# A start in source order, and two batches that take turns over the blocks of a hidden layer

## The chip, the cores and the metric

The kernel runs on one core of a Trainium2 chip. The metric is the device time of one execution in microseconds. The core's engines work beside each other, each through a queue of its own that it executes in order: TensorE (PE, matmuls; PEld in the profile is its weight load), VectorE (DVE), ScalarE (ACT), GpSimd (POOL) and SyncE (SP), which only issues transfers here. Results of PE land in PSUM, and DVE or ACT must copy them out before PE can use them as operands.

## The reference

Two softmax attentions and a two-layer network with Mish, cut to what matters (`_attn_ref`, `_moe_ref`):

```python
def sm_attn(qq, kk, vv):                     # q, k, v: 8 x 8 x 576 x 64;  p: 8 x 8 x 32 x 64
    s = scale * np.matmul(qq, kk.transpose(0, 1, 3, 2))
    s = s - np.max(s, axis=-1, keepdims=True)
    a = np.exp(s)
    a = a / (np.sum(a, axis=-1, keepdims=True) + 1e-09)
    return np.matmul(a, vv)
p_packed = sm_attn(p, k, v)                  # 32 packed rows for each batch and head
out = sm_attn(q, p_packed, p_packed)
x = out.transpose(0, 2, 1, 3).reshape(4608, 512)
h = x @ w_in                                 # 512 x 2048
g = h * np.tanh(softplus(h))
return g @ w_out                             # 2048 x 512
```

The two weights come as float64 and have to be made float32 on the chip.

## The kernel before

**Attention.** A `Batch` object holds one of the 8 batches; its 8 heads are worked in two groups g of four. `start` and `score` transpose p and k (PSUM tile `ps_kq`) and form the first scores `ps_s`; `exps` sums the exponentials into `rs`; `turn` transposes q into `qT`; `turn_weights` transposes the weights into `a1T`; `values` gives `ps_pp`, and `turn_values` its transpose `ppT`. `match` multiplies qT with ppT and transposes the result on DVE in squares of 32 (L240). `weigh` (L248 to L264) does the second softmax and leaves its transposed weights as a high and a low float32 part, `aT_hi` (ACT, L263) and `aT_lo` (DVE, L264). The generator `attention` yields these steps one by one, and the main loop slips a step between matmuls of the network.

**Folding.** The second attention's values are never formed: `packed_w(b, c)` multiplies ppT of batch b with chunk c of w_in (four chunks of 512 columns; PSUM tiles `ps_w`), which gives `wp_hi` (ACT, L349) and `wp_lo` (DVE, L350). The up-projection then multiplies aT with wp.

**Network.** The 2048 columns of the hidden layer are 16 blocks f of 128. A main-loop step t belongs to one block of one batch. `up(hf)` computes a half of the block's h transposed (288 of the batch's 576 rows): six matmuls into `ps_h`, three products (hi·hi, lo·hi, hi·lo) for each head group. ACT applies Mish (`g`, L391), and `halves` splits g into `g_hi`, `g_lo` on DVE (L400, L401). `down(grp, c)` adds the block's share to one of four accumulators `acc` (128 rows each) in three matmuls (L405 to L407). It runs two steps behind (`LAG`). The last 64 rows of a batch are kept in `g_rest` and multiplied with those of the next batch (`down_rest`).

**Weights.** `from_double` turns 128 x 512 float64 numbers to float32: SP stages them in `w_st` (three buffers), ACT makes the scaled high word and the low word (L295, L296), DVE joins them in four operations (L297, L298, L299, L302). There are 16 such pieces of w_in (`load_wi(c, m)`, four for each chunk) and 16 of w_out (`load_wo(i)`, which also splits them into `wo_hi` on ACT, L312, and `wo_lo` on DVE, L313). Chunks of w_in are written back as float32, and `fetch_wi` reads them again for later batches.

**Order.** PE executes in source order (`manual_schedule`). On the other engines a scheduler chooses the order when the kernel is built, and it is fixed from then on. The batches come one after the other: batch 0's attention runs first and alone, with the conversions placed among it, then t = 0 to 15 are batch 0's blocks, 16 to 31 batch 1's. Batch 1's attention is slipped in from t = 2 and completed at t = 14, where its first `packed_w` stands.

Of the kernel before, what the change touches and what calls it, by code (L numbers as in the profile page):

```python
# [10 lines left out]
I32 = mybir.dt.int32  # L11
# [8 lines left out]
W2K = 5  # L20

# [7 lines left out]
def body(  # L29
# [84 lines left out]
    def transposed(pool, src, g, dst):  # L114
        for i in range(NI):
            ps = psum(pool, [P, 4, R], "ps_kq")
            for h in range(4):
                nc.tensor.transpose(out=ps[:, h, :], in_=of_slot(src, g, h)[:, i, :], identity=ident[:R, :R])  # L118
            evacuate(dst[:, i, :, :], ps, i if pool is ps_acc else None)
            yield  # L120
# [15 lines left out]
    class Batch:  # L136
# [5 lines left out]
        def load(self):  # L142
            b = self.b
            self.k_t = [load_heads(k, b, g, "k_t") for g in range(2)]
            self.p_t = att.tile([P, 2, 2, D], F32, name="p_t", bufs=1)
            p_src = p[b].rearrange("(g h) n d -> (h n) g d", g=2)
            for u in range(2):
                nc.sync.dma_start(out=self.p_t[:, :, u, :], in_=p_src)
            self.q_t = [load_heads(q, b, g, "q_t") for g in range(2)]
            self.v_t = [load_heads(v, b, g, "v_t") for g in range(2)]  # L150
# [35 lines left out]

        def exps(self, gs):
# [41 lines left out]
        def turn(self, g, pool):  # L229
            self.qT[g] = att.tile([P, NI, 4, R], F32, name="qT", tag="T", bufs=2)  # L230
            yield from transposed(pool, self.q_t[g], g, self.qT[g])
# [11 lines left out]
        def weigh(self, gs):  # L243
            n = gs.stop - gs.start
            G = n * (S // NP)
            a2 = self.a2[:, gs].rearrange("a h g n -> a (h g) n")
            mx = stat.tile([P, 2 * (S // NP)], F32, name="mx2")[:, :G]
# [4 lines left out]
            nc.scalar.activation(out=a2, in_=a2, func=AF.Exp, scale=scale)  # L252
            sm = stat.tile([P, 2 * (S // NP)], F32, name="sm2")[:, :G]
# [14 lines left out]
        def attention(self):  # L268
# [15 lines left out]
            for g in range(2):  # L284
                yield from self.match(g, ps_a)
            self.weigh(slice(0, 2))

    def from_double(dst, src):


        x = src.rearrange("p (n t) -> p n t", t=2)
        low, high = x[:, :, 0], x[:, :, 1]
        bits = dst.bitcast(I32)
        r = wts.tile([P, dst.shape[1]], I32, name="wround", tag="w2k", bufs=W2K)
        nc.scalar.activation(out=dst, in_=high.bitcast(F32), func=AF.Copy, scale=F64_SCALE)  # L295
        nc.scalar.activation(out=r, in_=low.bitcast(U32), func=AF.Copy, scale=2.0 ** -29)  # L296
        nc.vector.tensor_scalar(out=dst, in0=dst, scalar1=F64_HIGH, scalar2=-F64_HIGH, op0=ALU.min, op1=ALU.max)  # L297
        nc.vector.tensor_scalar(out=bits, in0=bits, scalar1=3, scalar2=None, op0=ALU.logical_shift_left)  # L298
        nc.vector.scalar_tensor_tensor(  # L299
            out=bits, in0=high, scalar=-0x80000000, in1=bits, op0=ALU.bitwise_and, op1=ALU.bitwise_or  # L300
        )
        nc.vector.tensor_tensor(out=bits, in0=bits, in1=r, op=ALU.add)  # L302

    def staged(src):
        st = wts.tile([P, 2 * DO], I32, name="w_st", tag="wstage", bufs=3)
        nc.sync.dma_start(out=st, in_=src)
        return st

    def load_wo(i):
        w = wts.tile([P, DO], F32, name="wo32", tag="w2k", bufs=W2K)  # L310
        from_double(w, staged(w_out_v[:, i, :]))
        nc.scalar.copy(out=wo_hi[i], in_=w)  # L312
        nc.vector.tensor_tensor(out=wo_lo[i], in0=w, in1=wo_hi[i].bitcast(F32), op=ALU.subtract)  # L313
# [3 lines left out]
    def load_wi(c, m):  # L317

        g = m // 2
        if m % 2 == 0:  # L320
            wis[0, c, g] = wts.tile([P, 2, FC], F32, name="wi", tag="w32", bufs=4)
        from_double(wis[0, c, g][:, m % 2], staged(w_in_v[:, m, c * 2 * FC:(c + 1) * 2 * FC]))
        if m % 2:
            nc.sync.dma_start(out=w_in_f32[c][:, g], in_=wis[0, c, g])

    def fetch_wi(b, c):
        for g in range(2):
            wis[b, c, g] = wts.tile([P, 2, FC], F32, name="wi", tag="w32", bufs=4)
            nc.sync.dma_start(out=wis[b, c, g], in_=w_in_f32[c][:, g])

    def packed_w(b, c):
# [3 lines left out]
        for h in range(4):  # L335
            for g in range(2):
# [4 lines left out]
                    rhs=wis[b, c, g][row:row + D, h // 2, :],  # L341
# [24 lines left out]
    class Group:  # L366


        def __init__(self, b, f, wp, g_rest):
            self.b, self.f, self.wp, self.g_rest = b, f, wp, g_rest  # L370

        def tiles(self):
            self.act = moe.tile([P, MAIN], F32, name="g", tag="g", bufs=3)
            if self.f % 4 == 0:
                self.g_rest[self.b % 2].append(
                    moe.tile([P, 4, REST], F32, name=f"g_rest{self.b % 2}", bufs=2 if self.b % 2 else 5)
                )

        def up(self, hf):
# [12 lines left out]
            if m < HALF:  # L392
                nc.scalar.activation(
                    out=self.g_rest[self.b % 2][self.f // 4][:, self.f % 4, :], in_=ps[:, m:], func=AF.Mish
# [14 lines left out]
    def evac(acc, c):  # L409
        o = wts.tile([P, DO], F32, name="o", tag="w2k", bufs=W2K)  # L410
        if c % 2 == 0:
# [7 lines left out]
    def down(grp, c):  # L419
        b, f, g = grp.b, grp.f, grp.g  # L420
        if f == 0 and c == 0:
            accs[:] = [ps_acc.tile([P, DO], F32, name=f"acc{i}", tag="acc") for i in range(NCH)]
        down_one(accs[c], g[0], g[1], slice(c * P, (c + 1) * P), f, f == 0, f == NF - 1)
        if f < NF - 1:
            return
        o = evac(accs[c], c)
# [10 lines left out]
    def down_rest(grp):  # L437

        i = grp.f // 4
# [34 lines left out]
    with tc.manual_schedule(engines={mybir.EngineType.PE}):
# [3 lines left out]
        first.load()  # L478
        convert(2)
        first.start(ps_a)  # L480
        together(first.score(0, ps_acc))
        first.exps(slice(0, 1))
        together(first.score(1, ps_acc))
        first.exps(slice(1, 2))
        together(first.turn(0, ps_a))
        convert(2)
        together(first.turn_weights(0, ps_acc))
        together(first.turn(1, ps_a))
        together(first.turn_weights(1, ps_acc))
        together(first.values(0, ps_acc), first.values(1, ps_acc))  # L490
        together(first.turn_values(0, ps_a), first.turn_values(1, ps_a))
        together(first.match(0, ps_acc), first.match(1, ps_acc))
        for g in range(2):
            first.weigh(slice(g, g + 1))
        wps = {(0, 0): packed_w(0, 0)}
        convert(5)
# [3 lines left out]
        g_rest = None  # L500
        for t in range(n_groups + LAG):
            b, f = divmod(t, NF)
            grp = None
            if t < n_groups:
                if f == 0:
                    if b % 2 == 0:
                        g_rest = ([], [])
                if f == (0 if b else 2) and b + 1 < B:
                    gen = batches[b + 1].attention()
                if f == 10 and b + 2 < B:  # L510
                    batches[b + 2].load()
                grp = Group(b, f, wps[b, f // 4], g_rest)
# [3 lines left out]
            if b == 0:  # L516
                convert(2)
# [12 lines left out]
            if dn and dn.b % 2 == 1 and dn.f % 4 == 2:  # L530
                rest["g"] = split(dn.g_rest[0][dn.f // 4], dn.g_rest[1][dn.f // 4])
            if dn:
                down(dn, 3)
            if grp and f % 4 == 2:
                nb, nch = divmod(b * (NF // 4) + f // 4 + 1, NF // 4)
                if nb < B:
                    if nb > b:
                        together(gen)
                    wps[nb, nch] = packed_w(nb, nch)
                    if nb + (nch + 1) // 4 and nb + (nch + 1) // 4 < B:  # L540
                        fetch_wi(nb + (nch + 1) // 4, (nch + 1) % 4)
# [30 lines left out]
```

## Time and profile before

| what | value |
|---|---|
| median of 3 runs | 821.87 us (821.23 to 822.18) |
| the profiled execution | 822.64 us |
| its span | 820.9 us |
| busy: PE, DVE, ACT | 768.2, 420.6, 336.0 us |
| matmuls executed | 5584 |
| read and written in memory | 75.50 MB, 13.63 MB |

The span is the time from the profile's first event to its last; the execution's own time includes what lies around it. All instants (us) below are counted from the span's start. In rows of instructions the columns are start, duration, engine, line, operation, output and inputs, shapes, and in brackets the idle time ahead of it and what ended it. Rows of groups give busy time and mean ns of one. In rows of the chain of waits the second number is what that piece contributes.

### The profile page before, as it was taken

To read this page: it belongs to the slowest core of one execution; us is meant where nothing else is said; L and a number is where in the kernel's file an instruction comes from. 1 tells how busy PE (TensorE), PEld (TensorE's weight loads), DVE (VectorE), ACT (ScalarE), POOL (GpSimd) and SP (SyncE) were. 2 spreads that over 40 slices of the span, in tenths; PEclk is the share of its full clock that TensorE was granted. 3 is DMA by queue.
4 is the path that set the end of the run, shared out by engine and by line. 5 is a ranking of instruction groups with operands and counts; after the bars stand their busy time and mean duration, and the time that the engine had idled before them with its cause. 6 is when DMAs were issued, how large, how long until landed. Compare 5 with 4: busy or idle time off the path is not lost.

```text
span 820.9 us, 13745 instructions
## 1 busy us (share of the span) xinstructions
PE 768.2 (94%) x5584; PEld 610.4 (74%) x5584; DVE 420.6 (51%) x812; ACT 336.0 (41%) x766; POOL 0.7 (0%) x6
## 2 busy tenths in 40 slices
PE   6607789999999999999999999999999999999997
PEld 4406667787788787877778787877778787888886
DVE  4799895744373435544373435544373445533332
ACT  3557583435242353235242353335242353332221
POOL 0000000000000000000000000000000000000000
PEclk6557789999999999999999999999999999999999
DMA  9967673144311533144411433144311421131002
GB/s 256 287 226 231 207 243 95 52 139 138 110 52 52 143 95 111 52 138 139 110 52 52 132 107 111 52 137 140 110 52 52 122 67 53 52 103 52 1 1 64
DMA packets 43966, 90.02 MB, mean 110 GB/s; under 512 B 8576, under 2 KB 27008, under 8 KB 43904
## 3 DMA queue, kind: packets, MB, share of 16 engines
q1 hardware_dynamic: 43904, 89.15, 35.8%
q8 instruction: 44, 0.72, 0.4%
q14 instruction: 18, 0.15, 0.1%
HBM read 75.50 MB, written 13.63 MB: 109 GB/s over the span
## 4 chain that ended last, share of the span: by engine, by line
PE 88%; DMA 5%; DVE 4%; issue 1%; ACT 1%; SPq 0%; ACTq 0%
PE ps_h L388 25%; PE acc L405 16%; PE acc L407 14%; PE acc L406 14%; PE ps_kq L118 4%; DMA w_st<-in_moe_w_in_dram 4%; PE ps_w L338 4%; PE ps_s L127 3%; PE ps_rest L405 2%; PE ps_rest L407 2%; PE ps_rest L406 2%; PE ps_pp L209 1%; PE ps_a L200 1%; DMA k_t<-in_k_dram 1%; DMA w_st<-in_moe_w_out_dram 1%
## 5 line engine op out<-in xcount | busy, mean ns | idle before, releaser
L405 PE MATMUL acc<-wo_hi,g_hi 128*128 128x512 f32 x512 | 216.5, 423 | 0.0
L391 ACT ACTIVATE g<-ps_h 128x288 f32<-128x288 f32 (+1 forms) x256 | 98.5, 385 | 286.5 <-PE ps_h L388 250.5
L407 PE MATMUL acc<-wo_hi,g_lo 128*128 128x512 f32 x512 | 203.4, 397 | 0.0
L406 PE MATMUL acc<-wo_lo,g_hi 128*128 128x512 f32 x512 | 203.3, 397 | 0.0
L388 PE MATMUL ps_h<-aT_hi,wp_hi 128*128 128x288 f32 x512 | 159.3, 311 | 21.8 <-ACT aT_hi L263 21.1
L400 DVE CAST g_hi<-g 128x512 fp32r<-128x512 f32 x128 | 54.5, 426 | 239.7 <-ACT g L391 239.7
L388 PE MATMUL ps_h<-aT_lo,wp_hi 128*128 128x288 f32 x512 | 153.2, 299 | 1.9 <-DVE aT_lo L264 1.9
L388 PE MATMUL ps_h<-aT_hi,wp_lo 128*128 128x288 f32 x512 | 153.3, 299 | 0.0
L405 PEld LDWEIGHTS acc<-wo_hi,g_hi 128*128 128x128 f32 x512 | 97.4, 190 | 42.7 <-issue 20.4
L388 PEld LDWEIGHTS ps_h<-aT_hi,wp_hi 128*128 128x128 f32 x512 | 98.1, 192 | 39.6 <-ACT aT_hi L263 23.2
L407 PEld LDWEIGHTS acc<-wo_hi,g_lo 128*128 128x128 f32 x512 | 96.9, 189 | 23.7 <-DVE g_lo L401 0.2
L388 PEld LDWEIGHTS ps_h<-aT_lo,wp_hi 128*128 128x128 f32 x512 | 98.4, 192 | 11.3 <-DVE aT_lo L264 2.5
L406 PEld LDWEIGHTS acc<-wo_lo,g_hi 128*128 128x128 f32 x512 | 97.6, 191 | 8.6
L388 PEld LDWEIGHTS ps_h<-aT_hi,wp_lo 128*128 128x128 f32 x512 | 98.4, 192 | 0.0
L401 DVE TENSOR_TENSOR g_lo<-g,g_hi 128x512 fp32r<-128x512 f32 x128 | 88.2, 689 | 5.9
L350 DVE TENSOR_TENSOR wp_lo<-ps_w,wp_hi 128x512 fp32r<-128x512 f32 x64 | 41.3, 682 | 19.0 <-ACT wp_hi L349 19.0
L349 ACT CAST wp_hi<-ps_w 128x512 fp32r<-128x512 f32 x64 | 34.3, 588 | 32.8 <-PE ps_w L338 32.8
L338 PE MATMUL ps_w<-wi,ppT 64*32 64x512 f32 x512 | 35.7, 615 | 0.0
L118 PE MATMUL ps_kq<-ident,k_t 96*128 96x96 f32 x192 | 27.0, 273 | 9.0 <-issue 4.9
L118 PEld LDWEIGHTS ps_kq<-ident,k_t 96*128 96x128 f32 x192 | 23.1, 158 | 16.4 <-issue 6.4
L118 PE MATMUL ps_kq<-ident,q_t 96*128 96x96 f32 x192 | 26.6, 267 | 6.5 <-issue 2.9
L118 PEld LDWEIGHTS ps_kq<-ident,q_t 96*128 96x128 f32 x192 | 22.6, 154 | 13.1 <-issue 4.6
(81 smaller groups left out, 727.0 us busy)
## 6 DMA issues: line engine op xcount, KB each, us to landing
wi<-w_in_f SPq DMA_DIRECT2D x56, 512.0 KB, 4.5
k_t<-in_k_dram SPq DMA_DIRECT2D x32, 288.0 KB, 3.6
q_t<-in_q_dram SPq DMA_DIRECT2D x32, 288.0 KB, 4.8
v_t<-in_v_dram SPq DMA_DIRECT2D x32, 288.0 KB, 3.6
w_st<-in_moe_w_in_dram SPq DMA_DIRECT2D x16, 512.0 KB, 5.2
w_st<-in_moe_w_out_dram SPq DMA_DIRECT2D x16, 512.0 KB, 4.3
out_dram<-o SPq DMA_DIRECT2D x24, 192.0 KB, 2.5
w_in_f<-wi SPq DMA_DIRECT2D x8, 512.0 KB, 5.0
```

Of the source, the lines that this page charges most:

```text
L118: nc.tensor.transpose(out=ps[:, h, :], in_=of_slot(src, g, h)[:, i, :], identity=ident[:R, :R])
L127: nc.tensor.matmul(out=ps[u][h * NP:(h + 1) * NP, :], lhsT=packT[u * D:(u + 1) * D, h * NP:(h + 1) * NP], rhs=xT[u * D:(u + 1) * D, :, h, ...
L338: nc.tensor.matmul(out=ps[g][h * NP:(h + 1) * NP, :], lhsT=ppTb[row:row + D, g, h * NP:(h + 1) * NP], rhs=wis[b, c, g][row:row + D, h // 2 ...
L349: nc.scalar.copy(out=hi, in_=ps[g])
L350: nc.vector.tensor_tensor(out=lo, in0=ps[g], in1=hi.bitcast(F32), op=ALU.subtract)
L388: nc.tensor.matmul(out=ps, lhsT=w[:, fs], rhs=a[:, g, cs], start=(n == 0), stop=(n == 5))
L391: nc.scalar.activation(out=self.act[:, hf * HALF:hf * HALF + m], in_=ps[:, :m], func=AF.Mish)
L400: nc.vector.tensor_copy(out=hi, in_=self.act)
L401: nc.vector.tensor_tensor(out=lo, in0=self.act, in1=hi.bitcast(F32), op=ALU.subtract)
L405: nc.tensor.matmul(out=acc, lhsT=hi[:, cs], rhs=wh, start=start, stop=False)
L406: nc.tensor.matmul(out=acc, lhsT=hi[:, cs], rhs=wl, start=False, stop=False)
L407: nc.tensor.matmul(out=acc, lhsT=lo[:, cs], rhs=wh, start=False, stop=stop)
```

## The change

It has two parts. First, until the first block, DVE and ACT also run in source order. The source is rewritten for that: `score_now` takes the exponentials straight from PSUM, with the sums formed on the way (`accum_out`); `weigh` is split into `peak` and `weigh`; five weights `w0` to `w4` are fetched, made into words (ACT) and joined (DVE) at places written out by hand; k and p are loaded first, then `w0`, then q and v.

Second, the order of blocks is batch 0's blocks 0 to 7, then all 16 of batch 1, then batch 0's blocks 8 to 15; from batch 2 on all stays as it was. At the end of its first turn batch 0's four accumulators are copied to `part` tiles, and added at the end of the second one. Batch 1's attention is slipped in from t = 0 and completed at t = 6. Batch 1 uses chunks 0 and 1 of w_in while they are still there from batch 0. The conversions are issued at other steps. `g` has two buffers, not three, and `g_rest0` four, not five.

```diff
+TURNS = [(0, 0, 8), (1, 0, 16), (0, 8, 16)]
...
+        def score_now(self, g):
+            kT = att.tile([P, NI, 4, R], F32, name="kT", tag="T", bufs=2)
+            for _ in transposed(ps_acc, self.k_t[g], g, kT, ("ACT", "DVE", "ACT")):
+                pass
+            s_ps = scores(ps_a, self.pT[:, g, :], kT)
...
+                nc.scalar.activation(
+                    out=self.a1[:, g, u].rearrange("a i r -> a (i r)"), in_=s_ps[u], func=AF.Exp,
+                    bias=top, scale=scale, accum_out=sm[:, u:u + 1],
+                )
...
+    weights = [Weight(0, m) for m in range(4)] + [WeightOut(0)] + [Weight(1, m) for m in range(4)]
+    weights += [WeightOut(i) for i in range(1, 8)] + [Weight(2, m) for m in range(4)] + [WeightOut(8)]
+    weights += [Weight(3, m) for m in range(4)] + [WeightOut(i) for i in range(9, NF)]
...
+        with tc.manual_schedule(engines={mybir.EngineType.DVE, mybir.EngineType.Activation}):
+            first.load(False)
+            w0.fetch()
+            first.load_rest()
+            w1.fetch()
+            w2.fetch()
+            first.start(ps_a)
+            sums = [first.score_now(g) for g in range(2)]
+            w0.words()
+            w0.join()
+            for g in range(2):
+                first.sums_now(g, sums[g])
+                together(first.turn(g, ps_acc, ("ACT", "DVE", "ACT")))
+                together(first.turn_weights(g, ps_acc, ("ACT", "DVE")))
+            w1.words()
...
+            for g in range(2):
+                together(first.match(g, ps_acc))
+            first.peak(slice(0, 1))
+            w1.join()
+            w1.done()
+            first.peak(slice(1, 2))
+            w3.fetch()
+            w2.words()
+            first.weigh(slice(0, 1))
+            w2.join()
+            w4.fetch()
+            w3.words()
+            first.weigh(slice(1, 2))
+            w3.join()
+            w4.words()
+            w3.done()
+            wps = {(0, 0): packed_w(0, 0)}
+            w4.join()
+            w4.done()
...
-                if f == (0 if b else 2) and b + 1 < B:
+                b, f, begin, end = order[t]
+                if t in (0, 20):
+                    gen = batches[1 if t == 0 else 2].attention()
+                if b > 1 and f == 0 and b + 1 < B:
                     gen = batches[b + 1].attention()
...
-            if b == 0:
-                convert(2)
+            convert(4 if t == 0 else 2 if t < 4 else 1 if t == 4 or t > 7 else 0)
...
+            n = t // 4 + 1
+            if t % 4 == 2 and n < len(chunks):
+                nb, nch = chunks[n]
+                if nch == 0 and (nb, nch) != (0, 0):
+                    together(gen)
+                wps[nb, nch] = packed_w(nb, nch)
+                if n >= 7 and n + 1 < len(chunks):
+                    fetch_wi(chunks[n + 1][1])
```

In the changed source `up` is L444 to L449, `down` L461 to L463, `packed_w` L393 to L405, the join of a conversion L350 to L357, `weigh` L292 to L302 and `match` L243 to L274.

ScalarE around the first block. Before, from one exponential of batch 0's weigh chain to the next (`wo_`, `wi` and `wround` are pieces under conversion, `wp_hi` the first folded weights):

```order
L252 ACTIVATE a_428<-a_428 128x576
L295 ACTIVATE wi<-w_st 128x512
L296 ACTIVATE wround<-w_st 128x512
L295 ACTIVATE wo_568<-w_st 128x512
L296 ACTIVATE wround<-w_st 128x512
L349 CAST wp_hi<-ps_w_469 128x512
L349 CAST wp_hi<-ps_w_470 128x512
L252 ACTIVATE a_428<-a_428 128x576
```

The same engine now, up to the same two copies of wp_hi:

```order
L345 ACTIVATE wi<-w_st 128x512
L301 CAST aT_hi<-at 128x576
L345 ACTIVATE wo_458<-w_st 128x512
L346 ACTIVATE wround<-w_st 128x512 x2
L345 ACTIVATE wi<-w_st 128x512
L404 CAST wp_hi<-ps_w_479 128x512
L404 CAST wp_hi<-ps_w_480 128x512
```

The folding's copies moved behind both copies of aT, and behind the words of two pieces of chunk 1.

VectorE in batch 1's weigh chain. Before (`a_1436` are batch 1's second scores):

```order
L248 TENSOR_REDUCE mx_1519<-a_1436 128x36
L249 TENSOR_TENSOR a_1436<-a_1436,mx_1519 128x1152
L400 CAST g_hi<-g 128x512
L401 TENSOR_TENSOR g_lo<-g,g_hi 128x512
L254 TENSOR_REDUCE sm_1523<-a_1436 128x36
L255 TENSOR_SCALAR sm_1523<-sm_1523 128x36
L256 RECIPROCAL sm_1523<-sm_1523 128x36
L400 CAST g_hi<-g 128x512
L257 TENSOR_TENSOR a_1436<-a_1436,sm_1523 128x1152
L401 TENSOR_TENSOR g_lo<-g,g_hi 128x512
```

The same chain now, from the maxima to the sums' end (`a_1111` are the same scores):

```order
L282 TENSOR_REDUCE mx_1126<-a_1111 128x36
L283 TENSOR_TENSOR a_1111<-a_1111,mx_1126 128x1152
L405 TENSOR_TENSOR wp_lo<-ps_w_1143,wp_hi 128x512
L405 TENSOR_TENSOR wp_lo<-ps_w_1144,wp_hi 128x512
L350 TENSOR_SCALAR wi<-wi 128x512 x3
L353 TENSOR_SCALAR wi<-wi 128x512 x3
L292 TENSOR_REDUCE sm_1130<-a_1111 128x36
L354 SCALAR_TENSOR_TENSOR wi<-w_st,wi 128x512
L456 CAST g_hi<-g 128x512
L354 SCALAR_TENSOR_TENSOR wi<-w_st,wi 128x512 x2
L293 TENSOR_SCALAR sm_1130<-sm_1130 128x36
L357 ISA wi<-wi,wround 128x1024
```

Batch 1's folding and chunk 2's conversions moved in among the chain's steps, and g pairs moved out.

TensorE around batch 1's values. Before, in t = 9 (`acc` rows are the down-projection):

```order
L209 MATMUL ps_pp<-v_t,a1T 32x64 x24
L405 MATMUL acc_679<-wo_hi_100,g_hi 128x512
L406 MATMUL acc_679<-wo_lo_116,g_hi 128x512
L407 MATMUL acc_679<-wo_hi_100,g_lo 128x512
L405 MATMUL acc_680<-wo_hi_100,g_hi 128x512
L406 MATMUL acc_680<-wo_lo_116,g_hi 128x512
L407 MATMUL acc_680<-wo_hi_100,g_lo 128x512
L209 MATMUL ps_pp<-v_t,a1T 32x64 x24
```

Now, in t = 6:

```order
L461 MATMUL acc_723<-wo_hi_97,g_hi 128x512
L462 MATMUL acc_723<-wo_lo_113,g_hi 128x512
L463 MATMUL acc_723<-wo_hi_97,g_lo 128x512
L243 MATMUL ps_pp<-v_t,a1T 32x64 x48
L259 MATMUL ps_ppT<-ident,pp 128x128 x2
L130 MATMUL ps_s_1101<-qT,ppT 32x288 x4
L130 MATMUL ps_s_1102<-qT,ppT 32x288 x4
```

Values, their turns and the match stand back to back, with no block's work between them.

More of the change, by code (lines that the diff above doesn't have):

```diff
@@ L140, in __init__, with load @@
             self.b = b
-        def load(self):
+        def load(self, rest=True):
             b = self.b
@@ L227, in turn_values, with turn @@
             yield
-        def turn(self, g, pool):
+        def turn(self, g, pool, by=None):
             self.qT[g] = att.tile([P, NI, 4, R], F32, name="qT", tag="T", bufs=2)
-            yield from transposed(pool, self.q_t[g], g, self.qT[g])
+            yield from transposed(pool, self.q_t[g], g, self.qT[g], by)
         def match(self, g, pool):
@@ L241, in match, with peak @@
             yield
-        def weigh(self, gs):
-            n = gs.stop - gs.start
-            G = n * (S // NP)
+        def peak(self, gs):
             a2 = self.a2[:, gs].rearrange("a h g n -> a (h g) n")
+            G = a2.shape[1]
             mx = stat.tile([P, 2 * (S // NP)], F32, name="mx2")[:, :G]
@@ L285, in attention @@
                 yield from self.match(g, ps_a)
+            self.peak(slice(0, 2))
             self.weigh(slice(0, 2))
[L288 to L313, printed above, removed]
-    wis = {}
[L317 to L324, printed above, removed]
@@ new lines, in body, with __init__, fetch, done @@
+    class WeightOut(Weight):
+        def __init__(self, i):
+            self.i = i
+        def fetch(self):
+            self.st = wts.tile([P, 2 * FC], I32, name="w_st", tag="wstage", bufs=3)
+            nc.sync.dma_start(out=self.st, in_=w_out_v[:, self.i, :])
+            self.dst = wts.tile([P, DO], F32, name="wo32", tag="w2k", bufs=W2K)
+        def done(self):
+            nc.scalar.copy(out=wo_hi[self.i], in_=self.dst)
+            nc.vector.tensor_tensor(
+                out=wo_lo[self.i], in0=self.dst, in1=wo_hi[self.i].bitcast(F32), op=ALU.subtract
+            )
@@ L407, in down_one, with evac @@
         nc.tensor.matmul(out=acc, lhsT=lo[:, cs], rhs=wh, start=False, stop=stop)
-    def evac(acc, c):
-        o = wts.tile([P, DO], F32, name="o", tag="w2k", bufs=W2K)
-        if c % 2 == 0:
+    parts = {}
+    def evac(b, acc, c, last):
+        if not last:
+            o = parts[b, c] = wts.tile([P, DO], F32, name=f"part{b}{c}", bufs=1)
+        else:
+            o = wts.tile([P, DO], F32, name="o", tag="w2k", bufs=W2K)
+        if (b, c) in parts and last:
+            nc.vector.tensor_tensor(out=o, in0=acc, in1=parts[b, c], op=ALU.add)
+        elif c % 2 == 0:
             nc.scalar.copy(out=o, in_=acc)
@@ L420, in down @@
         b, f, g = grp.b, grp.f, grp.g
-        if f == 0 and c == 0:
+        if grp.first and c == 0:
             accs[:] = [ps_acc.tile([P, DO], F32, name=f"acc{i}", tag="acc") for i in range(NCH)]
-        down_one(accs[c], g[0], g[1], slice(c * P, (c + 1) * P), f, f == 0, f == NF - 1)
+        down_one(accs[c], g[0], g[1], slice(c * P, (c + 1) * P), f, grp.first, grp.last)
+        if not grp.last:
+            return
+        o = evac(b, accs[c], c, f == NF - 1)
         if f < NF - 1:
             return
-        o = evac(accs[c], c)
         a = c * P
@@ L477, in body @@
         first = batches[0]
-        first.load()
-        convert(2)
[L480 to L496, printed above, removed]
+        w0, w1, w2, w3, w4 = weights[:5]
+        del weights[:5]
+        with tc.manual_schedule(engines={mybir.EngineType.DVE, mybir.EngineType.Activation}):
[14 more added lines that the diff above has]
+            for g in range(2):
+                together(first.values(g, ps_a))
+            for g in range(2):
+                together(first.turn_values(g, ps_a))
+            for g in range(2):
+                together(first.match(g, ps_acc))
[16 more added lines that the diff above has]
+            w4.done()
         batches[1].load()
```

141 lines of the change are left out of this document (93 added, 48 removed).

## The prediction

> **What bounds the kernel now.** I read the page's slices first, then windows cut where TensorE changes its behaviour, then the waits between those cuts, then single rows.
>
> ```profile
> PE   6607789999999999999999999999999999999997
> DVE  4799895744373435544373435544373445533332
> PEclk6557789999999999999999999999999999999999
> ```
>
> A slice is 20.5 us. From the seventh on TensorE (PE) is full at full clock; before that VectorE (DVE) is the fuller one.
>
> ```profile
> 0.00:38.10 38.10, 26.03 (x256) 18.02 (x256) 23.59 (x59) 16.36 (x30) 0.70 (x6) 0.60 0.99 272
> 38.10:63.05 24.95, 2.07 (x5) 1.08 (x5) 22.70 (x47) 13.77 (x24) 0.00 (x0) 0.57 0.71 222
> 63.05:121.72 58.67, 45.63 (x255) 36.24 (x255) 53.26 (x115) 42.02 (x82) 0.00 (x0) 0.77 0.73 227
> 121.72:816.40 694.68, 694.49 (x5069) 555.02 (x5069) 320.39 (x592) 263.81 (x631) 0.00 (x0) 1.00 0.28 87
> ```
>
> Columns: stretch, its length, busy time of PE, weight loads, DVE, ScalarE (ACT), GpSimd, then granted clock, DMA share, GB/s. After 121.72 PE is busy for 694.49 of 694.68 us at clock 1.00: no change of order gains anything there, unless it opens a hole. In 38.10:63.05 DVE is busy for 22.70 of 24.95, in 63.05:121.72 for 53.26 of 58.67. So the start is bound by the transfers up to 38 (DMA share 0.99), then by DVE until 121.72, then by PE until the end. In figures, the time is the moment at which PE becomes full, plus the PE work left.
>
> ```profile
> PE ps_h L388 <- ACT aT_hi L263: 21.1, 2, 15.5
> PE ps_kq L118 <- issue: 7.8, 2, 4.9
> PE ps_kq L118 <- DVE wp_lo L350: 3.5, 1, 3.5
> ```
>
> ```profile
> 53.49 0.61 PE L388 MATMUL ps_h<-aT_hi,wp_hi 128*128 128x288 f32 x1 [15.50 <-ACT aT_hi L263]
> 61.96 0.61 PE L388 MATMUL ps_h<-aT_hi,wp_hi 128*128 128x288 f32 x1 [5.61 <-ACT aT_hi L263]
> 121.72 0.47 PE L118 MATMUL ps_kq<-ident,q_t 96*128 96x96 f32 x3 [1.05 <-DVE wp_lo L350]
> ```
>
> The PE waits of that stage (total, times, longest) and three of its PE rows: the first block's up-projection starts at 53.49, stalls again for the second head group until 61.96, and the last hole closes at 121.72, behind the first half of block 7 of batch 0.
>
> **What the change costs and brings.** It moves work among the three stages; PE executes the same matmuls.
>
> *The start.* Reordering k, p, q, v ahead of most weight staging, and taking the conversions out from ahead of the scores, brings batch 0's match forward.
>
> ```profile
> 42.05 0.47 DVE L240 STREAM_TRANSPOSE a<-ps_s 128x288 f32<-128x288 f32 x1
> 32.94 12.04 DMA w_st<-in_moe_w_in_dram
> 65.56 4.46 DMA w_st<-in_moe_w_out_dram
> ```
>
> Before, its last transpose ended at 42.5, with conversion operations between the four transposes. Following the new order with the row durations I get 32. But part of the 10.5 us is given back: the source order puts chunk 0's last three conversions into batch 0's weigh chain, the copy of aT_hi stands on ACT behind the words of chunk 1's first weight, and wp_hi behind those of its second. These wait for staging transfers, which took 12.04 us in the crowded start and 4.46 later. I take 54.8 for the first full up-projection, against 63 before: 8 us gained, between 0 (both transfers as slow as the 12.04) and 10.5.
>
> *The DVE stage up to batch 1's queries.* Batch 1 is now wanted at block step t=8, not t=16, so its whole attention stands in this stage.
>
> ```profile
> L297 DVE TENSOR_SCALAR wi<-wi 128x512 f32<-128x512 f32 x16 | 6.8, 423 | 7.4 <-ACT wi L295 7.3
> L298 DVE TENSOR_SCALAR wi<-wi 128x512 int32<-128x512 int32 x16 | 6.6, 418 | 0.0
> L299 DVE SCALAR_TENSOR_TENSOR wi<-w_st,wi 128x512 int32<-128x512 int32 x16 | 10.8, 683 | 0.0
> L302 DVE CUSTOM_DVE_ANT_0 wi<-wi,wround 128x1024 uint16<-128x1024 uint16 x16 | 10.8, 679 | 0.0
> L313 DVE TENSOR_TENSOR wo_lo<-wo,wo_hi 128x512 fp32r<-128x512 f32 x16 | 11.0, 686 | 1.0 <-ACT wo_hi L312 1.0
> L350 DVE TENSOR_TENSOR wp_lo<-ps_w,wp_hi 128x512 fp32r<-128x512 f32 x6 | 3.9, 686 | 0.0
> L181 DVE TENSOR_SCALAR a<-ps_s,top 128x288 f32<-128x288 f32 x8 | 3.7, 508 | 0.0
> L400 DVE CAST g_hi<-g 128x512 fp32r<-128x512 f32 x10 | 4.2, 425 | 3.7 <-ACT g L391 3.7
> L401 DVE TENSOR_TENSOR g_lo<-g,g_hi 128x512 fp32r<-128x512 f32 x10 | 6.9, 687 | 0.1
> ```
>
> ```profile
> 86.98 0.76 DVE L298 TENSOR_SCALAR wi<-wi 128x512 int32<-128x512 int32 x2
> 89.66 1.28 DVE L299 SCALAR_TENSOR_TENSOR wi<-w_st,wi 128x512 int32<-128x512 int32 x2
> ```
>
> A conversion is those four operations: 0.423 + 0.418 + 0.683 + 0.679 = 2.20 us when each waits for the one before, and 2 × 0.335 + 2 × 0.60 = 1.87 at the pace of neighbours that overlap (a second one of a pair adds 0.76 − 0.42 and 1.28 − 0.68). I take 1.87, since the order interleaves two of them nearly everywhere. From 54.4 to the pair that feeds the third block the order has 11 conversions (20.6), 8 wo_lo (5.5), 4 wp_lo (2.7), 4 g pairs (0.425 and 0.687, at the overlapping pace 0.34 + 0.60 = 0.94 each, 3.8) and batch 1's pT, maxima, subtractions and sums (6.5): 39.1 us, so 93.5. Nothing covers it: PE holds only its four blocks. Then ACT has to pass one more staged word (a landing like the 4.46, partly over) before it copies batch 1's qT: 97.2.
>
> *PE to batch 1's match.* Its prices at full clock are on the chain of waits:
>
> ```profile
> 123.70 0.33 PE ps_kq L118 x4
> 132.75 0.81 PE ps_pp L209 x48
> 140.78 0.65 PE ps_s L127 x16
> 145.82 1.07 PE ps_s L127 x16
> 148.48 0.80 PE ps_h L388 x6
> 149.28 0.24 PE acc L405
> 149.74 0.23 PE acc L407
> ```
>
> From there the PE order has 3 transpose sets (1.0), 5 up-projection halves (4.0), 9 down-projection triples (0.70 each, 6.3), 4 weight turns (priced like a transpose set, 1.3), values (2 × 0.81), pp turns (0.5) and match (0.65 + 1.07): 16.4. The passes PE to DVE and back between values, turns and match add some 1.3: M = 114.9.
>
> *Batch 1's weigh chain.* Before, it ran with cover to spare and had no conversions in it:
>
> ```profile
> 146.50 0.93 DVE L240 STREAM_TRANSPOSE a<-ps_s 128x288 f32<-128x288 f32 x2 [0.36 <-PE ps_s L127]
> 152.30 1.35 DVE L254 TENSOR_REDUCE sm<-a 128x36 f32<-128x1152 f32 x1 [1.02 <-ACT a L252]
> 160.52 0.76 DVE L264 TENSOR_TENSOR aT_lo<-at,aT_hi 128x576 fp32r<-128x576 f32 x1 [0.17 <-ACT aT_hi L263]
> ```
>
> From the match's end (145.82 + 1.07 = 146.9) to 161.3 it took 14.4 us, three g pairs among it. Now chunk 2's four conversions and one of w_out stand inside it: 5 × 1.87 = 9.4, plus two wp_lo with their wait (1.2), less two g pairs (1.9). That gives 23.1 us, so batch 1's aT_lo is ready at 138.0. PE meanwhile has only one folding of w_in (1.0), block 7 (1.6) and five down-projection triples (3.5) and their passes, some 7 us. It stands for about 16 us at t=8, where before it was busy. The converted weights are not wanted before t=14; they are merely ahead in DVE's queue.
>
> *The clock.* After a hole PE runs slowly:
>
> ```profile
> 80.60:86.30 5.70, 5.70 (x21) 5.02 (x22) 4.08 (x9) 3.66 (x7) 0.00 (x0) 0.50 0.42 117
> 107.69:113.60 5.91, 5.91 (x23) 5.22 (x24) 5.58 (x10) 5.79 (x10) 0.00 (x0) 0.50 0.65 225
> ```
>
> Each of these stretches follows a hole of about 3 us and ran at 0.50 for 5.7 to 5.9 us, a loss of 2.9. Of the new hole's I count 2.6, a part being in block 8's first half already. [...]
>
> *The sum.* At the end of block 8's first half PE has done more than before at 121.72: 12 up-projection matmuls 1.6, two transpose sets 0.7, values 1.6, four triples 2.8, match 1.7, weight turns 1.3, pp turns 0.4: 10.1 us. Block 8's half ends at 138.2. Span: 138.2 + (820.9 − 121.7) − 10.1 + 2.6 = 829.9; 1.74 us lie around the span (822.64 − 820.9), so 831.6 for such an execution. That execution stands 0.77 over the median of 821.87: 830.8.
>
> *Costed at nothing.* Four partial sums copied and added back: 8 DVE or ACT operations of about 0.6 us while PE is full (DVE is busy for 320 of 694 us there). Two g buffers instead of three: a block is about 4.4 us of PE, a g pair 0.94; if that cover went, each block would lose under 1 us. Fewer fetches of w_in on SP: DMA share 0.28 there.
>
> **Rivals.**
> *The start gains more.* DVE is idle for 14.5 of the first 38.10 us, waiting for transfers and scores. If source order removes that idle time, everything after moves with it, up to 830.8 − 14.5 = 816.3. For it: k and p now land before any weight. Against it: DMA is 0.99 busy, and chunk 0 must still land before the folding. It decides for faster from 10.5 us on (830.8 − 820.2).
> *The swap comes out even.* Start and chain both a little better: 8.9 us less, within 0.2% (1.6 us, about what a measurement here can tell from no change), 822.
> *Transfers in the chain.* ACT has two staged words ahead of batch 1's second aT_hi; if both landings are exposed, 2 × 4.46 = 8.9 more, 839.7. For it: DMA share 0.73 in 63.05:121.72. Against it: staging buffers come free early, since DVE is late.
>
> **How the numbers follow.** Forecast (a hole at t=8, 824 to 837) 0.66: M may move by 5 with the passes, conversions cost up to 5 × 0.33 = 1.7 more, the hole's clock 0.3 more or less. More gained at the start 0.17, even 0.08, transfers 0.09. Slower is then 0.75, same 0.08, faster 0.17. The range of 8 in 10 takes the forecast, the even case and the nearer parts of both other rivals: 818 to 840.
>
> **What would show it.** First up-projection near 55; PE wait at block 8's first matmul of 13 to 18 us, released by aT_hi or aT_lo of batch 1, with five conversions between its maxima and its last aT_lo; clock 0.50 for about 6 us after it; no hole later. The prediction is wrong if that wait is under 7 us, if block 8's half ends before 129.3 (138.2 − 8.9), or if a hole opens behind it: at the last two blocks of the turn, or where batch 2 begins.

## The result, and the profile after

The changed kernel takes 831.35 us (median of 4 executions, 830.48 to 833.58) against 822.02 us of the kernel before on the same chips: 1.0119 times as long, 95% interval 1.0103 to 1.0135. The forecast was 830.8. The profiled execution took 830.48 us with a span of 828.7.

The page's slices, as shown of before:

```profile
PE   6446974999999999999999999999999999999997
DVE  2779575695437544635273344634373344533332
PEclk9868795999999999999999999999999999999999
```

A slice is now 20.7 us. PE is fuller in the third and fifth slice (4 and 9 tenths, where it was 0 and 7), and has a new dent in the seventh, from 124 us on (4, where it was 9), where its clock falls to half as well (5, where it was 9). Windows cut at the places that the prediction names (stretch, length, busy times of PE, weight loads, DVE, ACT and POOL, clock, DMA share, GB/s):

```profile
0.00:38.10 38.10, 22.93 (x242) 17.31 (x242) 19.10 (x49) 12.40 (x27) 0.70 (x6) 0.94 0.84 237
38.10:54.50 16.40, 5.04 (x18) 1.35 (x19) 12.18 (x24) 6.95 (x12) 0.00 (x0) 0.50 0.37 113
54.50:97.00 42.50, 31.87 (x183) 23.70 (x183) 36.51 (x78) 30.95 (x60) 0.00 (x0) 0.80 0.65 213
97.00:121.00 24.00, 22.36 (x243) 16.46 (x242) 13.31 (x25) 10.95 (x22) 0.00 (x0) 1.00 0.26 75
121.00:136.20 15.20, 1.45 (x3) 0.78 (x3) 12.53 (x23) 5.31 (x12) 0.00 (x0) 0.55 0.63 213
136.20:142.40 6.20, 5.36 (x16) 4.46 (x17) 1.36 (x2) 2.09 (x5) 0.00 (x0) 0.50 0.20 70
...
150.00:824.00 674.00, 673.46 (x4845) 540.12 (x4843) 324.28 (x609) 263.64 (x630) 0.00 (x0) 1.00 0.29 89
```

Three things are to be seen. In 121:136.2 PE has 1.45 us of work and DVE is busy for 12.53 of 15.20: that is the hole. In 97:121 it is the other way round, PE at 22.36 of 24 and DVE at 13.31, waiting for it. And DVE is busy for only 19.10 of the first 38.10 us, where before it was 23.59. Behind 150 PE lacks 0.54 us in 674: the loss is all ahead of that.

The PE rows at these places, then four DVE and two ACT rows from batch 1's softmax (in brackets the idle time ahead of the row, and what ended it):

```profile
53.31 0.61 PE L444 MATMUL ps_h<-aT_hi,wp_hi 128*128 128x288 f32 x1 [0.68 <-ACT wp_hi L404]
...
95.38 0.55 PE L121 MATMUL ps_kq<-ident,q_t 96*128 96x96 f32 x4 [0.45 <-ACT qT L111]
...
111.80 1.14 PE L130 MATMUL ps_s<-qT,ppT 64*32 64x288 f32 x16 [0.15 <-DVE a L274]
...
131.70 0.61 PE L444 MATMUL ps_h<-aT_hi,wp_hi 128*128 128x288 f32 x1 [11.79 <-ACT aT_hi L301]
133.15 0.61 PE L444 MATMUL ps_h<-aT_lo,wp_hi 128*128 128x288 f32 x1 [0.85 <-DVE aT_lo L302]
...
136.86 0.61 PE L444 MATMUL ps_h<-aT_hi,wp_hi 128*128 128x288 f32 x1 [2.86 <-ACT aT_hi L301]
137.65 0.61 PE L444 MATMUL ps_h<-aT_lo,wp_hi 128*128 128x288 f32 x1 [0.19 <-DVE aT_lo L302]
...
138.30 0.63 PE L461 MATMUL acc<-wo_hi,g_hi 128*128 128x512 f32 x1
```

```profile
117.39 1.08 DVE L350 TENSOR_SCALAR wi<-wi 128x512 f32<-128x512 f32 x3
...
133.62 0.77 DVE L300 STREAM_TRANSPOSE at<-a 128x576 f32<-128x576 f32 x1
134.31 0.65 DVE L357 CUSTOM_DVE_ANT_0 wo<-wo,wround 128x1024 uint16<-128x1024 uint16 x1
136.84 0.76 DVE L302 TENSOR_TENSOR aT_lo<-at,aT_hi 128x576 fp32r<-128x576 f32 x1 [1.88 <-ACT aT_hi L301]
```

```profile
135.59 0.66 ACT L346 ACTIVATE wround<-w_st 128x512 int32<-128x512 uint32 x1 [3.94 <-DMA w_st<-in_moe_w_in_dram]
136.15 0.66 ACT L301 CAST aT_hi<-at 128x576 fp32r<-128x576 f32 x1
```

Batch 1's match ends at 111.80 + 1.14 = 112.94; between its maxima and its last aT_lo stand conversions from 117.39 to 134.96; the last copy of aT_hi stands on ACT behind a staged word, for which ACT waited 3.94 us; aT_lo is ready at 137.60. The copy's own input was ready at 133.62 + 0.77 = 134.39 and the copy began at 136.15, so that word delayed the softmax by 1.8 us. PE's waits at block 8's first half sum to 11.79 + 0.85 + 2.86 + 0.19 = 15.7 us.

### The profile page after: what moved, and what is told of

It is laid out like the page before. It is cut to its first block, busy times and chain, and to the rows that moved or that the text cites. A ratio compares the mean times of both kernels' runs of the same rounds, so it can differ in the third digit from the quotient of the medians.

```text
span 828.7 us, 13747 instructions
## 1 busy us (share of the span) xinstructions
PE 770.3 (93%) x5584; PEld 610.8 (74%) x5584; DVE 423.4 (51%) x814; ACT 335.2 (40%) x772; POOL 0.7 (0%) x6
## 4 chain that ended last, share of the span: by engine, by line
PE 83%; DVE 6%; DMA 5%; ACT 4%; issue 1%; SPq 0%; ACTq 0%; DVEq 0%
PE ps_h L444 23%; PE acc L461 15%; PE acc L463 13%; PE acc L462 13%; PE ps_kq L121 4%; PE ps_w L393 4%; DMA w_st<-in_moe_w_in_dram 3%; PE ps_s L130 3%; PE ps_rest L461 2%; PE ps_rest L463 2%; PE ps_rest L462 2%; PE ps_pp L243 2%; PE ps_a L234 1%; ACT wround L346 1%; DMA w_st<-in_moe_w_out_dram 1%
## 5 line engine op out<-in xcount | busy, mean ns | idle before, releaser
L461 PE MATMUL acc<-wo_hi,g_hi 128*128 128x512 f32 x512 | 215.6, 421 | 0.0
L463 PE MATMUL acc<-wo_hi,g_lo 128*128 128x512 f32 x512 | 204.1, 399 | 0.3 <-DVE g_lo L457 0.3
L456 DVE CAST g_hi<-g 128x512 fp32r<-128x512 f32 x128 | 54.5, 426 | 242.3 <-ACT g L447 242.2
L444 PE MATMUL ps_h<-aT_hi,wp_hi 128*128 128x288 f32 x512 | 159.2, 311 | 15.3 <-ACT aT_hi L301 14.7
L444 PE MATMUL ps_h<-aT_lo,wp_hi 128*128 128x288 f32 x512 | 152.9, 299 | 1.0 <-DVE aT_lo L302 1.0
L444 PE MATMUL ps_h<-aT_hi,wp_lo 128*128 128x288 f32 x512 | 152.9, 299 | 0.1
L461 PEld LDWEIGHTS acc<-wo_hi,g_hi 128*128 128x128 f32 x512 | 97.4, 190 | 41.8 <-issue 20.7
L444 PEld LDWEIGHTS ps_h<-aT_hi,wp_hi 128*128 128x128 f32 x512 | 97.9, 191 | 33.0 <-ACT aT_hi L301 15.4
L463 PEld LDWEIGHTS acc<-wo_hi,g_lo 128*128 128x128 f32 x512 | 97.1, 190 | 23.6 <-DVE g_lo L457 0.8
L444 PEld LDWEIGHTS ps_h<-aT_lo,wp_hi 128*128 128x128 f32 x512 | 97.9, 191 | 10.5 <-DVE aT_lo L302 1.7
L444 PEld LDWEIGHTS ps_h<-aT_hi,wp_lo 128*128 128x128 f32 x512 | 97.7, 191 | 0.7 <-DVE wp_lo L405 0.7
L393 PE MATMUL ps_w<-wi,ppT 64*32 64x512 f32 x512 | 40.1, 613 | 18.9 <-DVE wi L357 18.7
L405 DVE TENSOR_TENSOR wp_lo<-ps_w,wp_hi 128x512 fp32r<-128x512 f32 x64 | 41.5, 682 | 18.2 <-ACT wp_hi L404 18.1
L393 PEld LDWEIGHTS ps_w<-wi,ppT 64*32 64x32 f32 x512 | 6.5, 105 | 34.5 <-DVE wi L357 21.3
L111 ACT COPY kT<-ps_kq 128x384 f32<-128x384 f32 x42 | 20.1, 478 | 24.8 <-PE ps_kq L121 24.8
```

The costliest lines, as they stand in the source:

```text
L393: nc.tensor.matmul(out=ps[g][h * NP:(h + 1) * NP, :], lhsT=ppTb[row:row + D, g, h * NP:(h + 1) * NP], rhs=wis[c, g][row:row + D, h // 2, : ...
L405: nc.vector.tensor_tensor(out=lo, in0=ps[g], in1=hi.bitcast(F32), op=ALU.subtract)
L444: nc.tensor.matmul(out=ps, lhsT=w[:, fs], rhs=a[:, g, cs], start=(n == 0), stop=(n == 5))
L456: nc.vector.tensor_copy(out=hi, in_=self.act)
L461: nc.tensor.matmul(out=acc, lhsT=hi[:, cs], rhs=wh, start=start, stop=False)
L463: nc.tensor.matmul(out=acc, lhsT=lo[:, cs], rhs=wh, start=False, stop=stop)
```

## The experiments

All times are medians, all ratios against the kernel before run on the same chip. Where executions of one kernel scatter by some us, no difference below that is read from single profiles.

**One part at a time.** In `e1_start_only` the batches run whole, one after the other, with the order of conversions and the `g` and `g_rest0` buffers of before and two conversions at each step (four at the first). Cut:

```diff
-TURNS = [(0, 0, 8), (1, 0, 16), (0, 8, 16)]
+TURNS = [(0, 0, 16), (1, 0, 16)]
-            convert(4 if t == 0 else 2 if t < 4 else 1 if t == 4 or t > 7 else 0)
+            convert(4 if t == 0 else 2)
```

> Only the first part of the change: the start in source order, all batches whole, one after the other, conversions at two per block step from batch 0's first block (four at the first). Theory A, the prediction's term: the start gains some 8 us and everything behind it moves along: 812 to 815 us. Theory B: what counts is the vector engine's work left when the first block starts; in the changed kernel's trace that engine is busy for 31 us of the first 54.5, before for 39, and the new start saves only about 3.5 us of its work, so that some 4 us more are left and the gain is gone: 822 to 828 us.

It took 824.70 us, ratio 1.0037 (1.0022 to 1.0053). The start alone does not gain 8 us, it loses 3.1, as theory B expected; how it loses them is shown with e5.

In `e2_turns_only` the turns stay, and the start is that of the kernel before. Cut:

```diff
-        with tc.manual_schedule(engines={mybir.EngineType.DVE, mybir.EngineType.Activation}):
-            first.load(False)
-            ...
+        first.load()
+        convert(2)
+        first.start(ps_a)
+        ...
+        wps = {(0, 0): packed_w(0, 0)}
+        convert(5)
```

> Only the second part: batches 0 and 1 in turns, with the start of the kernel before (vector and scalar engine ordered by the scheduler, nine conversions placed among batch 0's attention). Theory A: the turns cost what was predicted and the start's 8 us are missing: 838 to 841 us. Theory B: the nine conversions done early leave less vector work behind the first block, so the match of batch 1 comes at the same time or earlier: 822 to 831 us.

It took 827.15 us, ratio 1.0062 (1.0045 to 1.0079): the turns alone lose 5.5 us. The two losses, 3.1 and 5.5, nearly add up to the whole change's 9.3. Its PE rows at block 8 show the same hole, a little smaller (12.0 us, where it was 15.7):

```profile
127.60 0.61 PE L444 MATMUL ps_h<-aT_hi,wp_hi 128*128 128x288 f32 x1 [7.33 <-ACT aT_hi L301]
129.94 0.61 PE L444 MATMUL ps_h<-aT_lo,wp_hi 128*128 128x288 f32 x1 [1.74 <-DVE aT_lo L302]
...
132.79 0.61 PE L444 MATMUL ps_h<-aT_hi,wp_hi 128*128 128x288 f32 x1 [2.00 <-ACT aT_hi L301]
...
134.36 0.61 PE L444 MATMUL ps_h<-aT_lo,wp_hi 128*128 128x288 f32 x1 [0.96 <-DVE aT_lo L302]
```

The match ends at 113.30, no earlier than in the changed kernel (112.94), though DVE has far less to do ahead of it:

```profile
54.50:97.00 42.50, 30.39 (x184) 24.12 (x185) 29.47 (x61) 25.38 (x49) 0.00 (x0) 0.72 0.39 116
```

DVE is busy here for 29.47 of 42.50 us, in the changed kernel for 36.51. But batch 0's first block waited for its second head group until 65.37, and from 66 to 97 PE is busy for 27.71 of 31.02 us, at a clock of 0.80. So less work left for DVE alone did not bring the match forward; here PE, which started late, takes about as long.

**The start: who stands idle.** `e5_start_scheduled` is e1 with one line changed:

```diff
-        with tc.manual_schedule(engines={mybir.EngineType.DVE, mybir.EngineType.Activation}):
+        with ExitStack():
             first.load(False)
```

> As e1_start_only (first part alone, 824.7 us against 821.6), but with the vector and scalar engines left to the scheduler in the start as well: the rewritten scores, the order of the loads and the places of the weights stay. Theory: e1 loses because engines that keep the source order stand idle in the start (23 of 54.5 us on the vector engine) where the scheduler puts conversions; with it back, and some 3.5 us of vector work saved by the new scores, 817 to 821 us. Rival: the order of the loads or the later weights cost it, whoever orders the engines: 823 to 827 us.

It took 818.02 us, ratio 0.9957 (0.9941 to 0.9974): 6.7 us less than e1 in medians, and faster than the kernel before. The first 54.5 us of three profiles, in the order before, e1, e5:

```profile
0.00:54.50 54.50, 26.64 (x257) 18.31 (x257) 37.74 (x89) 24.70 (x44) 0.70 (x6) 0.60 0.93 263
```

```profile
0.00:54.50 54.50, 27.36 (x260) 18.04 (x261) 31.33 (x72) 19.36 (x39) 0.70 (x6) 0.80 0.71 198
```

```profile
0.00:54.50 54.50, 24.84 (x257) 17.77 (x257) 38.16 (x92) 24.97 (x50) 0.70 (x6) 0.63 0.93 259
```

The third busy time is DVE's: 37.74, 31.33, 38.16. In source order DVE does 6.8 us less than in e5 by then, ACT 5.6 less, and the transfers run at a share of 0.71, not 0.93. By 54.5 us DVE has finished 10 conversions in the kernel before, 5 in e1 and 10 in e5 (counted by the last of their four operations).

What is not done in the start is done later, and PE waits for it. In e1 five conversions end between 121 and 140, where batch 1's values and match stand, and DVE is busy for 27.04 of the 29.00 us from 131 to 160. PE, full there in e5 (29.00), is busy for 25.72, with waits such as these:

```profile
137.28 0.33 PE L259 MATMUL ps_ppT<-ident,pp 128*128 128x128 f32 x1 [1.01 <-DVE pp L251]
...
141.35 0.69 PE L130 MATMUL ps_s<-qT,ppT 64*32 64x288 f32 x8 [1.73 <-DVE ppT L260]
```

These 3.3 us are about half of the difference; where the rest goes is not shown. The rewritten scores, loads and places are worth having together (3.7 us under before); the fixed order on the two engines takes 6.7 back.

**The hole at block 8.** `e3_chain_first` is the changed kernel with DVE and ACT in source order from t = 6 to 11 as well, so that batch 1's softmax comes ahead of what was slipped into it:

```diff
                 if nch == 0 and (nb, nch) != (0, 0):
+                    if t == 6:
+                        chain.enter_context(tc.manual_schedule(
+                            engines={mybir.EngineType.DVE, mybir.EngineType.Activation}))
                     together(gen)
```

> The changed kernel, with the vector and scalar engines in source order from batch 1's second softmax (t = 6) to t = 11 as well, so that this chain comes ahead of the conversions of chunk 2 and of the folding's copies; nothing is left out. Theory: the five conversions and two wp_lo in the chain cost about 10 us of the hole at t = 8; aT_lo of batch 1 comes near 126 to 128 instead of 137.6, and the time is 820 to 823 us. Rival: the chain is bound by its own steps and by transfers that come late anyway (the staged words ahead of aT_hi waited 3.9 us): no more than 4 us less, 827 to 831.

It took 822.47 us, ratio 1.0006 (0.9992 to 1.0020): nearly all of the loss is gone. The last aT_lo and the first row of block 8, with the ACT rows ahead of it:

```profile
123.52 0.76 DVE L302 TENSOR_TENSOR aT_lo<-at,aT_hi 128x576 fp32r<-128x576 f32 x1 [0.74 <-ACT aT_hi L301]
```

```profile
123.39 1.07 ACT L404 CAST wp_hi<-ps_w 128x512 fp32r<-128x512 f32 x2
124.48 1.28 ACT L447 ACT_TABLE_LOAD   x1
125.77 0.66 ACT L447 ACTIVATE g<-ps_h 128x288 f32<-128x288 f32 x2
```

```profile
126.23 0.61 PE L444 MATMUL ps_h<-aT_hi,wp_hi 128*128 128x288 f32 x1 [7.55 <-ACT g L447]
```

aT_lo is ready at 124.28, 13.3 us earlier. The match ended 1.2 us earlier too (111.72), so the softmax itself is 12.1 us shorter: 12.6 where it was 24.7. PE starts block 8 only at 126.23, since now block 7's Mish, which frees its PSUM buffer, stands behind the softmax, the folding's copies and a table load. So part of the gain turned into a new wait, as this row shows by its releaser: ACT g, not aT_hi.

`e6_old_start_chain_first` takes that wait away too, in the kernel of e2, with the order fixed from t = 6 to 11 again: the copies to wp_hi ahead of the exponential, wp_lo under it, and block 7's Mish ahead of the rest of the softmax. Cut:

```diff
+                    wps[nb, nch] = packed_w(nb, nch, late)
+                    batches[1].peak(slice(0, 2))
+                    for lo, s, hi in late:
+                        nc.vector.tensor_tensor(out=lo, in0=s, in1=hi.bitcast(F32), op=ALU.subtract)
...
                 grp.up(1)
+                if t == 7:
+                    batches[1].weigh(slice(0, 2))
```

> As e2_turns_only (turns with the old start, 827.2 us), with batch 1's second softmax ahead of the conversions, finer than in e3: the folding's ScalarE copies ahead of its exponential, its VectorE parts under it, and block 7's Mish before the chain's end, so that no PSUM buffer is waited for at block 8. Theory: in e2 the match ends at 113.3 and aT_lo at 135; with a chain of some 11 us the hole ends near 124.5 and the time is 815 to 819 us, under the kernel before. Rival: the hole moves to another wait, as in e3, where it went to Mish of block 7: 820 to 824 us.

It took 817.53 us, ratio 0.9951 (0.9933 to 0.9968). The hole is down to

```profile
117.08 0.40 PE L448 MATMUL ps_h<-aT_hi,wp_hi 128*128 128x288 f32 x1 [3.34 <-ACT aT_hi L301]
...
119.39 0.61 PE L448 MATMUL ps_h<-aT_hi,wp_hi 128*128 128x288 f32 x1 [0.99 <-ACT aT_hi L301]
```

So the turns are not slow by themselves: with the softmax ahead of conversions that nobody waits for yet, they are 4.2 us faster than the kernel before, and 9.6 faster than e2. The two profiles alone would say more than the edit did, because in e6's the match, ahead of everything that was changed, also ended 6.5 us earlier (e2: 113.30):

```profile
105.64 1.14 PE L130 MATMUL ps_s<-qT,ppT 64*32 64x288 f32 x16 [0.15 <-DVE a L274]
```

From there to the last aT_lo (119.38 + 0.76 = 120.14) the softmax takes 13.4 us, where in e2 it took 21.0. Of what the profiles show, these 7.6 us are the softmax; DVE and ACT had nearly the same order up to the match, and in 54.5:97 the clock was 0.84, not 0.72.

**Both mends.** `e8_both_parts_mended` has the start of e5 and the softmax of e6.

> The whole change with both mends: the start as in e5 (new scores, places and loads, but vector and scalar engine ordered by the scheduler) and batch 1's softmax ahead of the conversions as in e6. Theory: the two gains are separate (3.7 us in e5 and 4.2 in e6 against the kernel before) and add up as the two losses did (3.1 + 5.5 against 9.3): 812 to 816 us, under both e5 and e6. Rival: both take the same idle time of the vector engine in the first 54.5 us (busy for 38.2 us in both): 816 to 819 us, no better than either.

It took 817.25 us, ratio 0.9939 (0.9918 to 0.9960), with executions from 814.42 to 821.57. It is 5.2 us under the kernel before, not the 7.9 of the two gains together, and the intervals of e5, e6 and e8 overlap. The time fits the rival. Its reason does not fit as it stands: in e8's profile DVE is busy for 36.26 us of the first 54.5, not 38.2. And behind them, in e6 and e8:

```profile
54.50:97.00 42.50, 33.57 (x225) 26.92 (x226) 28.26 (x59) 25.55 (x53) 0.00 (x0) 0.84 0.44 125
```

```profile
54.50:97.00 42.50, 30.71 (x186) 24.07 (x187) 29.74 (x62) 25.49 (x51) 0.00 (x0) 0.72 0.48 144
```

DVE is busy for 28.26 and 29.74 of 42.50 us, where in e5 it is busy for 37.85. With the turns and a scheduled start DVE is not full behind the first block, so vector work saved in the start has little left to shorten. That is a reading of the profiles, and e8's is of its slowest execution (821.57); no run separates it from the rival. e8 is the fastest median of all, by no more than the scatter.

**A later deadline.** `e7_deadline_12` starts from e6 and gives batch 0 twelve blocks in its first turn, with chunk 2 converted before and the softmax of batch 1 in a fixed order at t = 8 to 11. Cut:

```diff
-TURNS = [(0, 0, 8), (1, 0, 16), (0, 8, 16)]
+TURNS = [(0, 0, 12), (1, 0, 16), (0, 12, 16)]
```

> As e6, but batch 0 keeps its first 12 blocks and batch 1 starts at t = 12; batch 1's attention is completed at t = 8, its softmax runs ahead of other vector work in t = 8 to 11, and chunk 2 is converted before. Theory: the hole is a matter of the deadline; with four blocks (17.6 us of tensor work) behind the match instead of one it closes, and the tensor engine is full from some 66 us on but for vector waits: 806 to 816 us. Rival: the conversions that batch 0's blocks 8 to 11 need (chunk 2, four of w_out) come on top before that, and the vector engine is the bound until t = 12: 818 to 826 us.

It took 835.18 us, ratio 1.0169 (1.0140 to 1.0198): both expectations missed. Its PE rows, and two ACT rows ahead of the last of them:

```profile
137.22 0.61 PE L448 MATMUL ps_h<-aT_hi,wp_hi 128*128 128x288 f32 x1 [5.15 <-ACT g L451]
...
148.69 0.80 PE L465 MATMUL acc<-wo_hi,g_hi 128*128 128x512 f32 x1 [4.54 <-DVE g_hi L460]
...
155.50 0.61 PE L448 MATMUL ps_h<-aT_hi,wp_hi 128*128 128x288 f32 x1 [4.21 <-ACT g L451]
```

```profile
152.32 0.68 ACT L347 ACTIVATE wround<-w_st 128x512 int32<-128x512 uint32 x1 [3.31 <-DMA w_st<-in_moe_w_in_dram]
...
155.04 0.65 ACT L451 ACTIVATE g<-ps_h 128x288 f32<-128x288 f32 x2
```

The fixed order that helped in e6 does harm here: Mish (`g`, L451) stands on ACT behind words and copies that wait for something else. `e9_deadline_12_scheduled` leaves these steps to the scheduler.

```diff
-                chain.enter_context(tc.manual_schedule(
-                    engines={mybir.EngineType.DVE, mybir.EngineType.Activation}))
                 together(gen)
```

> As e7 (batch 1 from t = 12; 835.2 us), but with the vector and scalar engines left to the scheduler behind the start. In e7 block 8's and block 10's Mish stood on the scalar engine behind words and softmax copies of the fixed order (holes of 5.2, 4.5 and 4.2 us from 137 to 155). Theory: that order alone made e7 slow, and with a later deadline no fixed order is needed: 808 to 818 us. Rival: the deadline is no cure, since the match comes at about the same block step after chunk 2's conversions and the vector engine is the bound: 820 to 830 us.

It took 826.35 us, ratio 1.0048 (1.0035 to 1.0060). The holes of e7 are gone, so 8.8 us between the medians (9.6 if each is taken against the kernel before on its chip) were that order's. The rest is what the rival expected:

```profile
54.50:97.00 42.50, 24.53 (x136) 18.72 (x137) 40.06 (x85) 27.99 (x54) 0.00 (x0) 0.86 0.74 241
```

DVE is busy for 40.06 of 42.50 us there, where in e2 it was 29.47: 13 conversions end in that stretch, chunk 2's four among them, where in e2 there are 6. A later deadline alone is no cure here, since it asks for more conversions ahead of it.

**The clock.** `e4_warm_hole` fills the hole with matmuls of zeros that nothing reads (10.88 and 2.84 us of them in its profile).

```diff
             for g in range(2):
+                if fill is not None:
+                    for _ in range((48, 12)[g]):
+                        nc.tensor.matmul(out=fill, lhsT=still, rhs=still, start=True, stop=True)
```

> The changed kernel, with 48 plain matmuls of zeros (about 11 us at full clock) put on the tensor engine ahead of block 8's first up-projection and 12 more (about 3 us) between its two head groups, in a tile that nothing reads. They stand in the hole, which stays. If the slow clock behind the hole costs the 2.6 us of the prediction, the time is 828.5 to 829.5 us and the clock is 1.00 behind 138. [...] If the slow stretch is covered by other waits: no change.

It took 832.19 us, ratio 1.0124 (1.0109 to 1.0139): no gain over the changed kernel's 1.0119. The clock behind the hole did stay up, but the profiled execution came to the hole later. Its windows:

```profile
54.50:97.00 42.50, 32.97 (x170) 24.95 (x171) 36.24 (x75) 29.31 (x55) 0.00 (x0) 0.65 0.66 207
...
140.77:147.00 6.23, 6.23 (x36) 5.44 (x35) 1.89 (x4) 2.92 (x7) 0.00 (x0) 1.00 0.01 3
```

Behind block 8's half (140.67 here, 138.30 in the changed kernel) the clock is 1.00, not 0.50, and 689.3 us are left, not 690.4. In 54.5:97, ahead of all that was changed, it was granted 0.65, against 0.80 in the changed kernel's profile, with the same instruction order on DVE and ACT. So the term shows as 1.1 us behind the hole and is not seen in the time; its size stays open.

## Why the prediction was right

- **First up-projection near 54.8.** It began at 53.31, behind wp_hi as the replayed order had it. But the word "gained" was wrong for this step, and so was the rival built on it, in which everything behind moves along. e1 shows that the start alone loses 3.1 us: DVE's idle time in the first 38.10 us rose from 14.5 to 19.0. The sum was not hurt, because it went on from DVE's remaining work in absolute time (54.4 + 39.1), and the conversions left over were in that 39.1. (The opening remark that DVE is the fuller engine ahead of the seventh slice does not hold for the first one, 4 tenths against PE's 6; nothing hangs on it.)
- **The DVE stage to 93.5, then one more staged word to 97.2.** DVE was busy for 36.51 of 42.50 us in 54.5:97, and 11 conversions ended there, as many as the sum has. PE's work behind it began at 95.38. The step came out about 2 us early, and M with it: 112.94, not 114.9. That DVE alone sets this moment is not shown: e2, with 7 us less vector work in the stretch, has its match at 113.30.
- **Batch 1's softmax: 23.1 us.** It took 137.60 − 112.94 = 24.7, with the conversions from 117.39 to 134.96 in it. The 1.6 us missed are about the 1.8 by which the staged word delayed the last aT_hi, a wait that the third rival had priced. e3 shows the mechanism: without the conversions and the folding in it, the softmax took 12.1 us less and the time fell by 8.9 us.
- **The hole: about 16 us.** 15.7, in four waits; the one at the first matmul is 11.79, under the 13 to 18 that were named for it. Both errors, −2.0 in M and +1.6 in the softmax, nearly cancel: block 8's half ended at 138.30, against 138.2. That it came this close is luck; the two steps were each off by about 2 us.
- **The clock: 2.6.** Rows of PE run at half rate from 136.86 to 142.72 (clock 0.50); the part behind 138.30 costs (142.72 − 138.30) / 2 = 2.2 us and the second head group 0.28 (from 137.65, behind its aT_lo, to 138.30 it took 0.65 us, in e4 at clock 1.00 it took 0.37); e4 shows only 1.1 of it. The slow stretch behind the wait is 5.9 us, as after the two holes of before that the prediction shows. It is not the same after each hole: in the changed kernel's own profile the one behind the 3.63 us hole at 67.73 is 3.4 us long (to 71.14, at clock 0.51). What sets the length is not shown.
- **Costed at nothing.** The partial sums, two g buffers and fewer fetches: PE lacks 0.54 us behind 150, so together they cost no more there. The four copies to `part` took 0.59 us each on ACT and 0.69 on DVE, the four additions 0.69.
- **The sum.** 829.9 for the span, 828.7 measured; 830.8 for the time, 831.35 measured.
- **The rivals.** "More gained at the start" had its condition backwards. "Transfers in the chain" happened in part: ACT waited 3.83, 2.03 and 3.94 us for staged words (at 125.86, 129.11 and 135.59), of which 1.8 us reached the last aT_hi and 1.2 held DVE at 129.80. The argument against it, that staging buffers come free early since DVE is late, was wrong way round: the join on DVE (L354) reads `w_st`, and between 100 and 140 SP's staging issues waited for that operation for 39.5 us in all, once for 23.4.

## What to carry to other kernels

When an engine is the bound for a stage, count its work left at the stage's start, not the moment at which its first result appears: a start that shows its first matmul at the same time with less done is a later finish (e1). But check that it still is the bound after the change: in e2 it was not. When a deadline is moved forward, look in the order for work that nobody waits for inside the chain that now has to meet it; taking it out was worth more here than the move itself. A fixed order helps where the chain is the only thing that anyone waits for, and hurts where it puts a step that frees a buffer behind a wait (e7), or leaves an engine idle that had other work (e1).

## What was not expected of the hardware

The granted clock in one and the same stretch with the same instruction order was 0.80 in one profile and 0.65 in another (54.5:97 of the changed kernel and of e4), and the match that follows came 3.2 us later (116.13, not 112.94); 1.0 us of that was there at the first block already (54.34, not 53.31). PE's longest holes there are 3.63 and 3.2 us. A hole much shorter than those that the prediction shows was followed by half rate too: in e1 one of 1.73 us (ahead of 141.35; behind it the matmuls of an up-projection start 0.24 us apart, at 133.3 it was 0.13), 2.3 us after PE had stood for 1.01 us at 137.28. Executions of one kernel scatter by 3 us here (830.48 to 833.58), and of e8 by 7.
